# Attention and two expert layers on one core: where a step's scores, first products and setup stand in the issue order

## The chip, the core and the metric

The kernel runs on one NeuronCore of a Trainium2 chip. It uses TensorE (PE; weight loads are listed apart as PEld), VectorE (DVE), ScalarE (ACT), GpSimd (POOL) and SyncE (SP), whose queue issues most of the transfers. Each engine works through its own instructions in order and waits where an operand, or a buffer that it is to write, is not free. The metric is the device time of one execution in microseconds, median of three runs.

## What is computed

Sizes: 2 batches, 8 heads, 576 positions, head width 64; then 1152 tokens of width 512.

```python
def _attn_ref(q, k, v, tau):
    scores = q @ k.T / sqrt(64)
    thresh = max(scores, -1) - tau
    scores = where(scores >= thresh, scores, -1e9)
    attn = exp(scores - max(scores, -1))
    attn = attn / (sum(attn, -1) + 1e-09)
    return attn @ v
def _moe_ref(x, w_in, w_out):              # 512 -> 2048 -> 512
    h = x @ w_in
    return where(h > 0, h, exp(min(h, 0)) - 1) @ w_out
def _moe2_ref(x, w_gate, w1, w2, capacity):  # 8 experts, 512 -> 1024 -> 512
    e = argmax(x @ w_gate); gate = softmax(x @ w_gate)[e]
    # each token goes to its expert while that has room
    out = gate * (relu(x @ w1[e]) @ w2[e])
```

The three are chained: attention, its heads laid side by side as x, the first layer, the expert layer.

## The kernel before, in words

Every operand of a product is split into two float16 parts, a rounded one and the remainder; a product is three matmuls (high by high, high by low, low by high) into one PSUM sum. The rounded part is ACT's copy, the remainder a subtraction on VectorE or GpSimd.

**Attention** works in 36 steps, four for each of the nine tiles of 128 rows, a step for a pair of heads. Tile 4 lies across the two batches. In a step VectorE takes the two maxima from the scores in PSUM (`emit_max`, L267) and makes two limits of them (`nb` L268, `th` L269); ACT takes the exponentials (L273); VectorE masks them against the limits and sums rows (L279); ACT and GpSimd split the pair (`emit_split`, L288, L289); SP transposes it by DMA (`emit_pt`, L294, tile `pt`); two steps later TensorE multiplies it with the values (`emit_pv`, L311: the old step's product). The scores of the next step (`emit_s`, L245) go into the same two score buffers, so each head's scores must wait for the mask of the same head. At a tile's last pair `emit_x` normalises it (L324 to L335) and transposes it into `xt`.

Key tiles (`prep_k`, L212 on ACT, L213 on VectorE) and value tiles (`prep_v`, L107 and L108) are loaded and split in the steps before their use, for batch 0 at the start and for batch 1 around steps 15 to 20, into five buffers each. Query tiles are split in the third step of a tile.

**Under the steps lies the first layer.** `conv` turns one of 32 pieces of its weights, which arrive as 64-bit numbers, into float16 parts: three VectorE operations (L358 to L362), two copies on ACT (L369, L370) and a GpSimd subtraction (L371). `CONV` puts one into steps 0 and 1 and two into steps 2 to 16. `piece` emits a chunk of products: a first product (`mm1_chunk`, L386, 48 matmuls into the one bank `mma`) or a second (`mm2_chunk`, L418, 12 matmuls into `mmb`). `FILL` sets how many pieces a step gets: none before step 7, three to step 17, two after; `piece(2)` allows second products alone, `piece(1)` takes a first product where it can. A first product's bank is read by `after` in three stages that `flush` advances: ACT (L400, L401), VectorE (L403), then ACT and GpSimd (L407, L408). Finished rows are routed to experts by `route`, which `slot` advances a stage at a time (x2_hi L442, x2_lo L447, and small VectorE operations); rows go out by an indirect DMA of GpSimd (L498).

Inside the loop the order on each engine is that of the program (`manual_schedule`). It is, for step i: old product; key loads and key split; value loads; `flush(1)`; maxima, exponentials; `flush(1)`; one conversion; `flush(1)`; pieces; mask of head 0, **scores of head 0**, mask of head 1; split and transpose; `settle`; second conversion; `emit_x`; `slot`; last piece; **scores of head 1**; value split; query split. Ahead of the loop stand `setup_first`, the first loads, key 0 and query 0, and `setup_rest` (L152: load and split of the gate weights, L153 to L155, constants on GpSimd and VectorE), then the scores of step 0.

**After the loop** a planner orders the instructions. A loop emits what is left of the first layer, with the first expert weights prepared among it; the last tile gets its own path (L546 to L613). Then come the eight experts (L671, L727, L700), their 32 weight pieces of 1 MB each loaded by SP (L622) and split by ACT and VectorE (L631, L634).

Of the kernel before, what the change touches and what calls it, by code (L numbers as in the profile page):

```python
# [7 lines left out]
F16 = mybir.dt.float16  # L8
# [12 lines left out]
P = 128  # L21
# [20 lines left out]
def kernel(  # L42
# [95 lines left out]
    lnsc = const.tile([P, 1], F32, name="lnsc")  # L138

# [12 lines left out]
    def setup_rest():  # L152
        nc.sync.dma_start(out=wg_f, in_=w_gate)  # L153
        nc.scalar.activation(out=wg[:, 0], in_=wg_f, func=ACTF.Copy, scale=SC)
        nc.vector.scalar_tensor_tensor(  # L155
            out=wg[:, 1], in0=wg_f, scalar=SC, in1=wg[:, 0], op0=ALU.mult, op1=ALU.subtract
        )
        nc.gpsimd.memset(lnsc, LN_GS)
        nc.gpsimd.memset(zero, 0.0)
        nc.gpsimd.memset(cum, 0.0)  # L160
        nc.gpsimd.memset(ones, 1.0)
        nc.gpsimd.iota(ev_i, pattern=[[1, E]], base=-E, channel_multiplier=0)
        nc.vector.tensor_copy(ev, ev_i)
        nc.gpsimd.iota(ids, pattern=[[P, NTILE]], base=0, channel_multiplier=1)
        nc.vector.tensor_scalar(ids, ids, OOB_ID, None, ALU.bitwise_xor)

        nc.gpsimd.affine_select(
            out=tri, in_=ones, pattern=[[1, P]], compare_op=ALU.is_gt, fill=0.0,
            base=0, channel_multiplier=-1,
        )  # L170
# [37 lines left out]
    def prep_k(b, j):  # L208
        k2 = raw_t.pop(("k", b, j))
        kt = attn.tile([P, 2, S], F16, name="kst", tag="kst", bufs=5)  # L210
        flat = kt.rearrange("p h s -> p (h s)")
        nc.scalar.activation(out=flat[0:D], in_=k2, func=ACTF.Copy, scale=SC)  # L212
        nc.vector.scalar_tensor_tensor(  # L213
# [4 lines left out]
    def prep_v(b, j):  # L218
        v1 = raw_t.pop(("v", b, j))
        vt = attn.tile([P, 2, VC], F16, name="vst", tag="vst", bufs=5)  # L220
# [99 lines left out]
    def emit_x(t_):  # L320
# [3 lines left out]
        nc.vector.tensor_scalar(r, rs, 1e-9, SC / XS, ALU.add, ALU.mult)  # L324
# [9 lines left out]
        xt[t_] = moe1.tile([P, 8, P], F16, name="xt", tag="xt", bufs=6)  # L334
# [44 lines left out]
    def mm1_chunk(t_, q, bank):  # L379
        ps = ps_m.tile([P, 512], F32, name=f"mm{bank}", tag=f"mm{bank}")  # L380
# [42 lines left out]
    def mm2_done(ps, t_, q0, q1):  # L423
# [3 lines left out]
        elif q0 == 0:  # L427
            x2acc[t_] = shared.tile([P, DM], F32, name="acc", tag="acc", bufs=3)
# [378 lines left out]
    def pick2():  # L807
# [5 lines left out]
        for t_ in range(NTILE - 1):  # L813
# [5 lines left out]
            if ready("o", q + QG - 1, 6) and (q or aside < 3):  # L819
                return t_, q + QG  # L820
# [9 lines left out]
    def piece(first=0):  # L830
# [5 lines left out]
        if b is None or (a is not None and first < 2):  # L836
            q = nq1[a]
            nq1[a] += 1
            bank = "a"
            flush()  # L840
            evac.append(mm1_chunk(a, q, bank))
# [15 lines left out]
    cur, done = {}, []  # L857

# [12 lines left out]
    with tc.manual_schedule():  # L871
# [10 lines left out]
        prep_k(0, 0)  # L882
        prep_q(0)
        setup_rest()
        sc = {z: emit_s(0, z) for z in range(2)}
        for i in range(NSTEP + LAG):
# [3 lines left out]
            nf = FILL[i]  # L890
            if i >= LAG:
# [6 lines left out]

            for b, base in ((0, 0), (1, 4 * NPAIR)):
# [3 lines left out]
                if 0 <= jk < NPAIR:  # L903
                    prep_k(b, jk)
                jv = i + 1 - LAG - base
# [4 lines left out]
            flush(1)  # L910
            if on:
                lim = emit_max([sc[z] for z in range(2)])
                for z in range(2):
                    emit_exp(sc[z], lim[0], pair_p[i], z)
            flush(1)
            if nc_:
                conv_next()
            flush(1)
            for _ in range(nf - 1):
                piece(2) or (nc_ and not evac and piece(1))  # L920
            if on:
                for z in range(2):
                    emit_mask(sc[z], lim[1], pair_p[i], z, t_, 2 * j + z)
                    if z == 0 and i + 1 < NSTEP:
                        sc[0] = emit_s((i + 1) // NPAIR, (2 * i + 2) % H)
                emit_split(i)
                emit_pt(i)
            settle()
            for _ in range(nc_ - 1):
                conv_next()  # L930
            if i >= LAG and (i - LAG) % NPAIR == NPAIR - 1:
                emit_x((i - LAG) // NPAIR)
                x_at[(i - LAG) // NPAIR] = i
            slot()
            if nf:
                piece(1)
            if i + 1 < NSTEP:
                sc[1] = emit_s((i + 1) // NPAIR, (2 * i + 3) % H)
            for b, base in ((0, 0), (1, 4 * NPAIR)):
                jv = i + 1 - LAG - base  # L940
                if 0 <= jv < NPAIR:
                    prep_v(b, jv)
# [37 lines left out]
    k = 0  # L980
    while sum(nq1) < NQ * NTILE or sum(nq2) < NQ * (NTILE - 1) or evac:
# [143 lines left out]
```

## Time and profile before

| | us |
|---|---|
| median of three runs | 633.44 |
| lowest and highest run | 630.64, 633.81 |
| profiled execution | 635.48 |
| its span, first to last instruction | 633.7 |
| PE busy | 452.4 (71%) |
| DVE busy | 405.0 (64%) |
| ACT busy | 354.4 (56%) |
| POOL busy | 267.8 (42%) |

Busy time leaves out register, branch, semaphore and DMA-issuing instructions. The shares are means over stages with different limits, so they are read stage by stage further down. The span is shorter than the execution, since it runs from the first to the last instruction.

### The profile page before, as it was taken

The numbers are of one execution on the slowest core, as the hardware profiler recorded it, in microseconds if no ns is written. First come the engines' busy times: TensorE is split into PE (matmuls) and PEld (weight loads), VectorE is DVE, ScalarE is ACT, GpSimd is POOL, SyncE is SP. The second block draws the span as 40 slices with busy tenths as digits, with TensorE's granted clock in tenths as the row PEclk, the third lists the DMA queues.
The fourth block names the chain that finished last, engine by engine and source line by source line (L and its number), as shares of the span: only waits on it lengthen the run. The fifth ranks groups of instructions, "written<-read, shape, count | busy, mean of one in ns | idle before, by whom it ended". The sixth has DMA issues, their size and how long they took to land.

```text
span 633.7 us, 13023 instructions
## 1 busy us (share of the span) xinstructions
PE 452.4 (71%) x5343; PEld 367.6 (58%) x5343; DVE 405.0 (64%) x768; ACT 354.4 (56%) x511; POOL 267.8 (42%) x193
## 2 busy tenths in 40 slices
PE   1123345754654678995899899976989999787793
PEld 0012234444523636773677677654889999787681
DVE  2588795894596576785779578366534567654541
ACT  2346456565556456654576756366538665675541
POOL 1225446364455163453555455321234244533342
PEclk9999997776878789997999899989999999998898
DMA  6465677477456665853589747496617897887731
GB/s 190 140 147 159 171 185 182 113 185 200 104 139 173 162 151 141 193 124 72 109 179 212 118 94 102 88 291 223 228 45 206 245 283 242 241 276 210 236 67 41
DMA packets 150771, 105.59 MB, mean 167 GB/s; under 512 B 135209, under 2 KB 135209, under 8 KB 146608
## 3 DMA queue, kind: packets, MB, share of 16 engines
q1 hardware_dynamic: 148064, 99.94, 62.1%
q0 software_dynamic: 2640, 4.74, 2.3%
q8 instruction: 44, 0.72, 0.5%
q14 instruction: 23, 0.19, 0.1%
HBM read 60.06 MB, written 12.68 MB: 115 GB/s over the span
## 4 chain that ended last, share of the span: by engine, by line
DVE 38%; DMA 22%; PE 16%; ACT 11%; issue 10%; POOL 2%; SPq 1%; DVEq 0%; POOLq 0%; ACTq 0%
DMA stg<-in_w_dram 8%; PE mma L386 8%; DVE pp L279 7%; DVE m L267 6%; DMA out_dram<-y,ix 5%; DVE cvp L359 4%; DVE we L634 3%; DVE cvp L358 3%; PE mmb L418 3%; DMA pt<-phl 3%; DMA yr<-yt 2%; DVE kst L213 2%; PE s L245 2%; ACT we L631 2%; DVE cvp L362 2%
## 5 line engine op out<-in xcount | busy, mean ns | idle before, releaser
L386 PE MATMUL mma<-xt,wi 128*128 128x128 f16 x1728 | 116.2, 233 | 33.1 <-DVE gf L403 33.1
L386 PEld LDWEIGHTS <-wi 128*128 128x128 f16 x1728 | 111.2, 106 | 37.1 <-issue 25.4
L245 PE MATMUL s<-kst,qst 128*128 128x288 f16 (+1 forms) x320 | 56.2, 333 | 72.5 <-DVE pp L279 63.4
L418 PE MATMUL mmb<-wo,g 128*128 128x512 f16 x384 | 95.8, 403 | 12.1 <-DVE x L447 6.5
L634 DVE SCALAR_TENSOR_TENSOR we<-stg,we 128x1024 f16<-128x1024 f32 x64 | 78.3, 1256 | 38.9 <-ACT we L631 38.7
L289 POOL TENSOR_TENSOR phl<-pp,phl 128x1152 f16<-128x1152 f32 x36 | 85.3, 2371 | 14.8 <-POOL g L408 9.2
L631 ACT ACTIVATE we<-stg 128x1024 f16<-128x1024 f32 x64 | 64.4, 1049 | 41.5 <-DMA stg<-in_w_dram 40.7
L408 POOL TENSOR_TENSOR g<-gf,g 128x512 f16<-128x512 f32 x36 | 41.7, 1157 | 102.6 <-ACT g L407 102.5
L273 ACT ACTIVATE pp<-s,nb,escale 128x576 f32<-128x576 f32 x72 | 55.9, 827 | 49.2 <-DVE nb L268 49.1
L245 PEld LDWEIGHTS <-qst 128*128 128x128 f16 (+1 forms) x320 | 29.4, 112 | 91.6 <-DVE pp L279 53.3
L671 PE MATMUL mm<-xs,we 128*128 128x196 f16 x768 | 69.6, 253 | 14.3 <-DVE g L754 4.8
L671 PEld LDWEIGHTS <-we 128*128 128x128 f16 x768 | 66.7, 100 | 16.2 <-DVE we L634 8.1
L418 PEld LDWEIGHTS <-g 128*128 128x128 f16 x384 | 37.5, 103 | 56.7 <-issue 22.3
L311 PE MATMUL pv<-vst,pt 128*128 128x64 f16 (+3 forms) x1080 | 48.5, 208 | 30.7 <-DVE xf L327 11.9
L267 DVE TENSOR_REDUCE m<-s 128x1 f32<-128x576 f32 x72 | 52.0, 750 | 27.0 <-PE s L245 26.7
L311 PEld LDWEIGHTS <-pt 128*128 128x128 f16 (+1 forms) x1080 | 46.2, 108 | 37.1 <-issue 30.5
L684 POOL TENSOR_TENSOR ht<-rf,ht 128x392 f16<-128x392 f32 x32 | 35.7, 1126 | 74.3 <-issue 38.7
L727 PE MATMUL mm<-ht,we 128*128 128x196 f16 x672 | 58.5, 248 | 2.0 <-DVE yt L738 1.3
L727 PEld LDWEIGHTS <-we 128*128 128x128 f16 x672 | 57.4, 98 | 2.4 <-issue 2.3
L279 DVE SCALAR_TENSOR_TENSOR pp<-s,th,pp 128x576 f32<-128x576 f32 x72 | 55.9, 813 | 4.4 <-ACT pp L273 4.3
L288 ACT ACTIVATE phl<-pp 128x1152 f16<-128x1152 f32 x36 | 41.9, 1165 | 12.7 <-DVE pp L279 12.7
L400 ACT ACTIVATE ef<-mma 128x512 f32<-128x512 f32 x36 | 21.4, 594 | 46.3 <-PE mma L386 42.1
(123 smaller groups left out, 599.5 us busy)
## 6 DMA issues: line engine op xcount, KB each, us to landing
stg<-in_w_dram SPq DMA_DIRECT2D x32, 1024.0 KB, 6.4
cst<-in_w_in_dram SPq DMA_DIRECT2D x16, 512.0 KB, 4.4
cst<-in_w_out_dram SPq DMA_DIRECT2D x16, 512.0 KB, 4.4
disp<-zero SPq DMA_DIRECT2D x6, 771.0 KB, 4.7
qraw<-in_qt_dram SPq DMA_DIRECT2D x9, 512.0 KB, 3.4
vraw<-in_vb_dram SPq DMA_DIRECT2D x8, 320.0 KB, 5.7
kraw<-in_kt_dram SPq DMA_DIRECT2D x8, 288.0 KB
out_dram<-zero SPq DMA_DIRECT2D x1, 2304.0 KB
```

Of the source, the lines that this page charges most:

```text
L245: nc.tensor.matmul(s[a:z, half, 0:288], q2[:, pas, h, a:z], kst[b, h // 2][:, h % 2, half * 288:(half + 1) * 288], start=(pas == 0), stop= ...
L267: nc.vector.tensor_reduce(out=m[:, z:z + 1], in_=sc[z], axis=AX.XY, op=ALU.max)
L273: nc.scalar.activation(out=pp[:, z].rearrange("p (a c) -> p a c", a=2), in_=s, func=ACTF.Exp, bias=nb[:, z:z + 1], scale=escale,)
L279: nc.vector.scalar_tensor_tensor(out=e, in0=s, scalar=th[:, z:z + 1], in1=e, op0=ALU.is_ge, op1=ALU.mult, accum_out=rsum[t_][:, h:h + 1],)
L289: nc.gpsimd.tensor_tensor(out=d[:, 1], in0=flat, in1=d[:, 0], op=ALU.subtract)
L311: nc.tensor.matmul(o[a:e, h:h + w // D, :].rearrange("p h d -> p (h d)"), q[:, ph * 9 + blk, a:e], vt[:, vh, c:c + w], start=(blk == 4 and ...
L386: nc.tensor.matmul(ps[:, o * P:(o + 1) * P], w[:, wh, kk, :], xt[t_][:, xh * 4 + kk, :], start=(k_ == 0), stop=(k_ == 11),)
L418: nc.tensor.matmul(ps, gt[t_, q][:, gh, o, :], w[:, wh, :], start=(first and o == 0 and n == 0), stop=(last_ and o == QF - 1 and n == 2),)
L631: nc.scalar.activation(out=w[:, 0, part], in_=t[:, part], func=ACTF.Copy, scale=SC)
L634: nc.vector.scalar_tensor_tensor(out=w[:, 1, part], in0=t[:, part], scalar=SC, in1=w[:, 0, part], op0=ALU.mult, op1=ALU.subtract)
L671: nc.tensor.matmul(ps[:, o * n:(o + 1) * n], w[:, wh, kk % 2, f * P:(f + 1) * P], t[:, xh * 4 + kk, :], start=(k_ == 0), stop=(k_ == 11),)
L727: nc.tensor.matmul(ps[:, o * n:(o + 1) * n], w[:, wh, f % 4, j * P:(j + 1) * P], h2[:, gh, f, :], start=(f == 0 and n_ == 0), stop=(f == 7 ...
```

## The change

- **Scores.** Head 0's scores stay behind its mask, and head 1's now follow head 1's mask directly, ahead of everything else on TensorE.
- **Pieces.** Ahead of the masks only second products are emitted (`piece(2)`, without the fallback to a first product); one first product, `piece(1)`, ends the step. The stages of its reader are emitted once behind the exponentials and then, all that are left, behind the split and the transpose.
- **Keys and values.** Both get six buffers. The key split's ACT half stays at the head of a step, its VectorE half moves behind the exponentials. Values are loaded and split one step earlier.
- **Setup.** `setup_rest` moves from ahead of the first scores to the end of step 0, behind its split, transpose and `settle`. It gets two more constants, `eps` and `xsc`, which L324 reads in place of immediates.
- **Order of the rest.** The second conversion of a step moves behind `emit_x`.
- **After attention** a first product takes one of five rotating banks (`ps_e`, `mm`) in place of `mma`.
- **Buffers.** `xt` goes from six to four, `acc` from three to two, and two tiles at most (not three) may have a partial second product set aside.

```diff
@@ setup_rest
         nc.gpsimd.memset(lnsc, LN_GS)
+        nc.gpsimd.memset(eps, 1e-9)
+        nc.gpsimd.memset(xsc, SC / XS)
@@ prep_k (prep_v: bufs=5 to bufs=6)
-        kt = attn.tile([P, 2, S], F16, name="kst", tag="kst", bufs=5)
+        kt = attn.tile([P, 2, S], F16, name="kst", tag="kst", bufs=6)
         flat = kt.rearrange("p h s -> p (h s)")
         nc.scalar.activation(out=flat[0:D], in_=k2, func=ACTF.Copy, scale=SC)
+        yield
         nc.vector.scalar_tensor_tensor(
@@ emit_x (xt: bufs=6 to bufs=4; acc in mm2_done: bufs=3 to bufs=2)
-        nc.vector.tensor_scalar(r, rs, 1e-9, SC / XS, ALU.add, ALU.mult)
+        nc.vector.tensor_scalar(r, rs, eps, xsc, ALU.add, ALU.mult)
@@ mm1_chunk
-        ps = ps_m.tile([P, 512], F32, name=f"mm{bank}", tag=f"mm{bank}")
+        ps = bank()
@@ pick2
-            if ready("o", q + QG - 1, 6) and (q or aside < 3):
+            if ready("o", q + QG - 1, 6) and (q or aside < 2):
@@ piece
-            evac.append(mm1_chunk(a, q, bank))
+            evac.append(mm1_chunk(a, q, m1_bank[0]))
@@ ahead of the loop
+    m1_bank = [lambda: ps_m.tile([P, 512], F32, name="mma", tag="mma")]
...
-        prep_k(0, 0)
+        for _ in prep_k(0, 0):
+            pass
         prep_q(0)
-        setup_rest()
-        sc = {z: emit_s(0, z) for z in range(2)}
+        sc = [emit_s(0, z) for z in range(2)]
@@ the loop
+            halves = []
             for b, base in ((0, 0), (1, 4 * NPAIR)):
...
                 if 0 <= jk < NPAIR:
-                    prep_k(b, jk)
-                jv = i + 1 - LAG - base
+                    halves.append(prep_k(b, jk))
+                jv = i - base
...
-            flush(1)
+            for g in halves:
+                next(g)
             if on:
-                lim = emit_max([sc[z] for z in range(2)])
+                lim = emit_max(sc)
                 for z in range(2):
                     emit_exp(sc[z], lim[0], pair_p[i], z)
+            for g in halves:
+                next(g, None)
             flush(1)
             if nc_:
                 conv_next()
-            flush(1)
             for _ in range(nf - 1):
-                piece(2) or (nc_ and not evac and piece(1))
+                piece(2)
             if on:
                 for z in range(2):
                     emit_mask(sc[z], lim[1], pair_p[i], z, t_, 2 * j + z)
-                    if z == 0 and i + 1 < NSTEP:
-                        sc[0] = emit_s((i + 1) // NPAIR, (2 * i + 2) % H)
+                    if i + 1 < NSTEP:
+                        sc[z] = emit_s((i + 1) // NPAIR, (2 * i + 2 + z) % H)
                 emit_split(i)
                 emit_pt(i)
+            flush()
             settle()
-            for _ in range(nc_ - 1):
-                conv_next()
             if i >= LAG and (i - LAG) % NPAIR == NPAIR - 1:
                 emit_x((i - LAG) // NPAIR)
                 x_at[(i - LAG) // NPAIR] = i
+            if i == 0:
+                setup_rest()
+            for _ in range(nc_ - 1):
+                conv_next()
             slot()
             if nf:
                 piece(1)
-            if i + 1 < NSTEP:
-                sc[1] = emit_s((i + 1) // NPAIR, (2 * i + 3) % H)
             for b, base in ((0, 0), (1, 4 * NPAIR)):
-                jv = i + 1 - LAG - base
-                if 0 <= jv < NPAIR:
-                    prep_v(b, jv)
+                if 0 <= i - base < NPAIR:
+                    prep_v(b, i - base)
@@ after the loop
+    m1_bank[0] = lambda: ps_e.tile([P, 512], F32, name="mm", tag="mm")
```

## Rows read from the trace of the kernel before

**Rows 1.** Windows, four stretches: length, busy us per engine (instructions), clock, DMA share, GB/s.

```profile
0.00:99.60 99.60, 30.35 (x274) 20.91 (x274) 71.05 (x120) 47.53 (x63) 36.88 (x33) 1.00 0.60 163
99.60:245.24 145.64, 88.61 (x964) 66.33 (x964) 99.89 (x172) 80.33 (x117) 68.78 (x46) 0.79 0.64 163
245.24:391.48 146.24, 131.00 (x1769) 98.45 (x1770) 109.38 (x250) 93.09 (x128) 77.57 (x46) 0.96 0.65 128
391.48:470.75 79.27, 65.86 (x850) 52.91 (x849) 42.07 (x118) 40.68 (x63) 23.05 (x20) 0.94 0.64 180
```

**Rows 2.** Waits of the whole span: who waited for whom, us in total, times, longest.

```profile
PE s L245 <- DVE pp L279: 63.4, 19, 16.0
...
PE mma L386 <- DVE gf L403: 33.1, 10, 5.3
...
DVE m L267 <- PE s L245: 26.7, 13, 5.5
```

**Rows 3.** Timeline, first masks of steps 0, 1, 6, 7, 8, 18, 35: start, us.

```profile
26.41 0.81 DVE L279 SCALAR_TENSOR_TENSOR pp<-s,th,pp 128x576 f32<-128x576 f32 x1
...
36.63 0.81 DVE L279 SCALAR_TENSOR_TENSOR pp<-s,th,pp 128x576 f32<-128x576 f32 x1
...
91.23 0.81 DVE L279 SCALAR_TENSOR_TENSOR pp<-s,th,pp 128x576 f32<-128x576 f32 x1
...
99.60 0.81 DVE L279 SCALAR_TENSOR_TENSOR pp<-s,th,pp 128x576 f32<-128x576 f32 x1
...
116.16 0.81 DVE L279 SCALAR_TENSOR_TENSOR pp<-s,th,pp 128x576 f32<-128x576 f32 x1
...
245.24 0.82 DVE L279 SCALAR_TENSOR_TENSOR pp<-s,th,pp 128x576 f32<-128x576 f32 x1 [0.24 <-ACT pp L273]
...
391.48 0.82 DVE L279 SCALAR_TENSOR_TENSOR pp<-s,th,pp 128x576 f32<-128x576 f32 x1 [0.25 <-ACT pp L273]
```

**Rows 4.** Groups by line, whole span: busy us, mean ns, idle before and its releaser.

```profile
L267 DVE TENSOR_REDUCE m<-s 128x1 f32<-128x576 f32 x72 | 52.0, 750 | 27.0 <-PE s L245 26.7
...
L403 DVE SCALAR_TENSOR_TENSOR gf<-ef,mma 128x512 f32<-128x512 f32 x36 | 24.6, 682 | 17.5 <-ACT ef L401 17.4
...
L268 DVE TENSOR_SCALAR nb<-m,cmul 128x2 f32<-128x2 f32 x36 | 15.5, 430 | 1.3
...
L213 DVE SCALAR_TENSOR_TENSOR kst<-kraw,kst 64x1152 f16<-64x1152 f32 x8 | 13.0, 1626 | 22.7 <-ACT kst L212 22.6
```

**Rows 5.** Timeline of the start, SP's queue and ACT: start, us, idle before.

```profile
8.12 0.47 SPq L195 DMA_DIRECT2D kraw<-in_kt_dram  x1
...
19.93 0.23 ACT L154 ACTIVATE wg<-wg_f 128x32 f16<-128x32 f32 x1 [12.16 <-DMA wg_f<-in_w_gate_dram]
...
31.64 2.84 SPq L294 DMA_TRANSPOSE pt<-phl  x1
```

**Rows 6.** Chain of waits, first load: start, us.

```profile
1.27 4.24 DMA kraw<-in_kt_dram
```

**Rows 7.** Timeline, step 7's second first product: start, us, idle before.

```profile
106.36 5.28 PE L386 MATMUL mma<-xt,wi 128*128 128x128 f16 x48 [5.14 <-DVE gf L403]
```

**Rows 8.** Timeline near 120 us, GpSimd's subtraction and VectorE's two limits.

```profile
119.68 2.36 POOL L289 TENSOR_TENSOR phl<-pp,phl 128x1152 f16<-128x1152 f32 x1
...
121.14 0.93 DVE L268 TENSOR_SCALAR nb<-m,cmul 128x2 f32<-128x2 f32 x1
...
121.98 1.20 DVE L269 TENSOR_SCALAR th<-m,cadd 128x2 f32<-128x2 f32 x1
```

**Rows 9.** Timeline of TensorE, the old step's product in steps 24 and 25.

```profile
300.90 1.03 PE L311 MATMUL pv<-vst,pt 128*128 128x128 f16 x27
...
308.07 1.03 PE L311 MATMUL pv<-vst,pt 128*128 128x128 f16 x27
```

**Rows 10.** Timeline of ACT at step 22: start, us, idle before.

```profile
290.44 0.60 ACT L442 ACTIVATE x<-mmb 128x512 f16<-128x512 f32 x1 [8.52 <-DMA disp<-x,slot_i]
```

**Rows 11.** Waits from 405 to 470 us: us in total, times, longest.

```profile
PE mma L386 <- DVE gf L403: 7.8, 4, 3.5
```

More of the change, by code (lines that the diff above doesn't have):

```diff
@@ L138 @@
     lnsc = const.tile([P, 1], F32, name="lnsc")
+    eps = const.tile([P, 1], F32, name="eps")
+    xsc = const.tile([P, 1], F32, name="xsc")
     def setup_first():
@@ L219, in prep_v @@
         v1 = raw_t.pop(("v", b, j))
-        vt = attn.tile([P, 2, VC], F16, name="vst", tag="vst", bufs=5)
+        vt = attn.tile([P, 2, VC], F16, name="vst", tag="vst", bufs=6)
         split(vt[:, 0], vt[:, 1], v1, SC, "dve")
@@ L333, in emit_x @@
         nc.gpsimd.tensor_tensor(out=xh[:, 1], in0=xf, in1=xh[:, 0], op=ALU.subtract)
-        xt[t_] = moe1.tile([P, 8, P], F16, name="xt", tag="xt", bufs=6)
+        xt[t_] = moe1.tile([P, 8, P], F16, name="xt", tag="xt", bufs=4)
         nc.sync.dma_start_transpose(out=xt[t_], in_=xh.rearrange("p a s -> p (a s)"))
@@ L427, in mm2_done @@
         elif q0 == 0:
-            x2acc[t_] = shared.tile([P, DM], F32, name="acc", tag="acc", bufs=3)
+            x2acc[t_] = shared.tile([P, DM], F32, name="acc", tag="acc", bufs=2)
             nc.scalar.activation(out=x2acc[t_], in_=ps, func=ACTF.Copy)
@@ L838, in piece @@
             nq1[a] += 1
-            bank = "a"
             flush()
-            evac.append(mm1_chunk(a, q, bank))
+            evac.append(mm1_chunk(a, q, m1_bank[0]))
             g_at[a, q] = step[0] + 1
```

## The prediction

> **What bounds the kernel now.** I first cut the span at the starts of the first mask of steps 0, 1, 6, 7, 8, 18 and 35 [rows 3] and read the busy time of each engine between the cuts [rows 1]. The reader is to see four stages with different limits, and an expert stage behind them. In steps 0 to 7 VectorE works 71.1 of 99.6 us and TensorE 30.4: the vector chain decides. In steps 7 to 18 (145.6 us for 11 steps, 13.2 each) nobody is full: VectorE 99.9, TensorE 88.6, at a granted clock of 0.79. In steps 18 to 35 (146.2 us, 8.6 each) TensorE is near full with 131.0. In the tail up to the first expert product TensorE has 65.9 of 79.3 us.
>
> Then I read who waits [rows 2]. TensorE waits 63.4 us for masks before scores and 33.1 us for the vector step that frees the only bank of a first product; VectorE waits 26.7 us for scores. The second stage shows how these hang together: step 7 puts two first products around the scores. The second of them begins 5.1 us late, since its bank is freed behind VectorE's work, then runs at half the full clock (5.28 us for 48 products, against about 2.7 at 2.4 GHz, half of it) [rows 7], and the second head's scores stand behind it on TensorE. The step from 99.60 to 116.16 takes 16.6 us, while the step before it, with two weight conversions and no product, takes 8.4 [rows 3].
>
> **Start and steps 0 to 7.** Now the gate-weight load is last in SP's first batch, and ACT's copy of it at 19.93 us holds everything [rows 5]. After the change it goes behind step 0. The second key tile is issued at 8.12 [rows 5]; a key load took 4.24 us [rows 6], so it is there at 12.4. From the release at 19.93 to the mask at 26.41 passed 6.5 us; the maxima and their two limits (two of 0.75 us [rows 4], the limits some 0.3 more) no longer come behind the keys, the gate copy is 0.2, so the first mask starts near 12.4 + 4.5 = 16.9, 9.5 earlier. But the moved step is not free. On SP it stands behind step 0's transpose, which is issued 5.2 us after the mask begins (26.41 to 31.64) and holds the queue 2.84 [rows 3, 5]; with a landing of 4.24 [rows 6] the gate weights are there at 16.9 + 5.2 + 2.8 + 4.2 = 29.1. ACT and VectorE wait there in order, and behind them the value pieces, which the change also puts one step earlier (0.7 on ACT, 0.8 on VectorE, estimates by length from the key piece of 1.63 [rows 4]), and the next maxima. The 6.5 us then serve again, less the key copy on ACT (about 1.1, now beside the maxima), plus these 1.5: the second mask at 36.0, against 36.63 [rows 3]. So 9 of the 9.5 us are given back. A landing in half the time would leave 2 more, in twice the time cost 4. I take 1 gained: 4.24 is the nearest row, but for 18 times the bytes. GpSimd's nine small setup operations, two more than before, fill its wait behind step 0's subtraction. Step 4 has no value piece any more: it falls from about the 10.9 that steps 1 to 6 average to the plain 8.4 of step 6 now [rows 3], a gain of 2.4; the tile's normalisation, now ahead of a conversion and so ahead of GpSimd's subtraction, gives 0.6 (an estimate). **Stage: -4**, bounds +4 and -8.
>
> **Steps 7 to 18.** With at most one first product in a step, always behind both scores, its bank's reader runs straight behind the masks and no score stands behind a product. That leaves VectorE's loop. Base: nine steps at 8.37 [rows 3]; the last two lack one and two conversions of some 2.05 (8.37 less two maxima of 0.75 [rows 4], two masks that follow each other as fast, and 1.2 of limits with their waits, halved): 6.3 and 4.3. Sum 85.9. Eight steps carry a product's reader, 0.68 [rows 4], and 0.6 because its subtraction on GpSimd lies before the limits: 10.2. Three normalisations, 1.1 each by the size of their one long operation: 3.3. Four key pieces at 1.63 [rows 4]: 6.5; each of them waited for ACT at the head of its step and now lies under the exponentials, and with six buffers the copy need not wait for the scores of the oldest keys. Two value pieces with their waits, 1.8 each: 3.6. One accumulator addition and a row split, 2, and collisions with GpSimd's query pieces, 3, are estimates. Total 114.5 against 145.6. **Stage: -31.** Were TensorE at half clock throughout, a first product of 5.28 [rows 7] and twice the 1.03 of an old step's product [rows 9], and as much again for the scores, are 9.5, still beside VectorE's 9.65; only the three steps with second products would grow, by some 10 together. Bounds: -38 (no collision, no wait of limits) and -11 (every step 2 us more).
>
> **Steps 18 to 35.** TensorE's round is 7.17 us, from one step's old product to the next's [rows 9]; no product is added or taken, so it stays. What changes is the slack. Before, the first maximum was taken under the first product. Now maxima follow the masks at once and the limits come due about 2.2 us after them (a product's reader and two maxima [rows 4]), while GpSimd's 2.36-us subtraction of the step runs: in step 0 the transpose behind it was issued 3.7 us after the two masks [rows 3, 5], so it runs from 1.3 to 3.7. The rows show what that means: a limit begun at 121.14, in the last us of such a subtraction, took 0.93 and ended with it, and the next limit then took 1.20, until the following GpSimd operation ended [rows 8]. So the first limit ends 3.9 us after the masks, the second 5.0, behind the product's subtraction, and two masks of 0.75 spacing end at 6.6. Add 0.15 for ACT. 6.75 against 7.17 leaves 0.4, and whatever VectorE does between masks and maxima now counts against it. Eight steps with routing, value or query work then cost about 0.5 more: **+4**, bounds -8 (the old order's own excess halves) and +17 (1 us in every step). The long wait of step 22 (ACT 8.5 us for a dispatched row [rows 10]) stays: the same tiles are routed in the same steps, and fewer transposed tiles or accumulators bind nowhere, since their last reader is at least six steps earlier.
>
> A page of the Trainium skill speaks against this part: SBUF — State Buffer, section Who interferes with whom, says that a two-port VectorE operation and a GpSimd operation exclude each other, the later one blocked until the earlier has finished, and that issue order decides. The trace agrees as to the exclusion, 0.93 and 1.20 us for limits of which the first kind takes 0.43 on the mean of 36; as to the order, the first limit slipped in between two GpSimd operations here.
>
> **Tail and experts.** Counting the pieces through, attention ends with 29 first products done, not 30, so the tail gets one more: +2.7. Taking five rotating banks there removes the 7.8 us that products waited for their bank's reader [rows 11]. **-5**; bounds +3 (none of it removed) and -11 (all 13.4 us of TensorE's idle time gone [rows 1]). The weight loads start when attention ends and so move with it. The order of this part is a planner's; what it does with the experts I set at 0, within 6 either way. Constants from tiles instead of immediates: nothing, since the limits, of the same operation, read their scalar from a tile already.
>
> **How the numbers follow.** -4 - 31 + 4 - 5 = -36 against a profiled execution of 635.5 (633.7 of span, 1.8 around): 599.5. The median of the runs is 2.0 below it: **597.5**, in its own range 588 to 607. Chance 0.50.
>
> **Rivals.** (a) VectorE's limits bind the third stage: if the product's subtraction on GpSimd goes ahead of the first limit as well, as the 1.20 us of the second show it can [rows 8], the loop is 6.75 + 1.2 = 7.95, 0.78 over TensorE's round, 13 us in 17 steps: 610. For it: GpSimd is at work 77.6 of 146 us there [rows 1]; against it, the limit that slipped in [rows 8]. By the page's rule on issue order, named above, it would come out so. 0.18. (b) Only stalls that hang on the second product go: the second stage keeps other waits (loads, ACT's order), 20 us of the 31 stay: 617. For it: all waits of first products for their bank are 33.1 us, in the whole kernel [rows 2], so that 31 asks for nearly everything; against it, the plain step of 8.4 with the same loads [rows 3]. That is also how it looks if the change doesn't do what it says. 0.12. (c) The tail loses all its idle time, and the third stage runs at TensorE's round: 6 and 10 more: 581. 0.13. (d) Slower: without a product between the scores, TensorE's cover of the mask chain is gone; when everything that VectorE does between masks and limits also waits for GpSimd, the third stage's loop sets the pace. It eats the gain of 40 elsewhere from 7.17 + 40/17 = 9.5 us per step on; at 9.8 it gives 638. Against it: that needs 3 us more than the loop I find. 0.07.
>
> A difference of 0.5%, 3 us, is about what a measurement of this kernel can tell from none. Faster 0.91, same 0.02 (the far end of (b)), slower 0.07. The range of 8 in 10 takes in (c), (a) and most of (b): 580 to 618.
>
> **What would show it.** First masks of steps 0, 1, 7, 18 and 35 near 17, 36, 95.5, 210 and 360; the gate copy near 29; waits of first products for their bank near nil, and of maxima for scores too; the mean of the first limit up from 0.43 [rows 4] to over 1 us. Wrong is the forecast if the second stage stays over 125 us, if the third passes 160, or if the experts take 10 us more than their 163.

## The result and the profile after

The changed kernel takes 599.15 us (median of four runs, 597.22 to 601.08), the kernel before 633.11 on the same occasion (630.64 to 633.81): ratio 0.947, 95% interval 0.943 to 0.951. The profiled execution took 600.27, its span 598.6. The forecast was 597.5, in a range from 580 to 618.

The first view is the windows of after, cut at the first masks of steps 7, 18 and 35 and at the first expert product, as [rows 1] cut before (columns: stretch, its length, busy time and count of each engine, granted clock, DMA share, GB/s):

```profile
core 0: us, PE busy (x) PEld busy (x) DVE busy (x) ACT busy (x) POOL busy (x), PEclk, DMA share, GB/s
0.00:93.21 93.21, 26.33 (x226) 18.40 (x226) 69.97 (x120) 47.39 (x63) 36.86 (x35) 0.82 0.61 175
93.21:207.07 113.86, 77.51 (x899) 54.63 (x900) 102.45 (x172) 77.96 (x113) 67.61 (x45) 0.86 0.75 198
207.07:359.11 152.04, 136.92 (x1835) 101.80 (x1836) 116.30 (x248) 89.40 (x127) 76.96 (x46) 0.97 0.58 131
359.11:432.29 73.18, 65.91 (x897) 53.99 (x896) 43.29 (x120) 42.77 (x68) 26.70 (x21) 0.95 0.64 193
432.29:598.60 166.31, 140.73 (x1491) 132.44 (x1488) 83.68 (x112) 92.89 (x143) 60.43 (x49) 0.93 0.71 196
```

The second stage lost 31.8 of its 145.6 us, and VectorE is now busy for 90% of it, against 69%. The third stage got 5.8 us longer. The other stages moved by -6.4 (start), -6.1 (tail) and +3.4 (experts).

The cuts, and two steps more, are the first masks of steps 0, 1, 7, 8, 18 and 35 (start, duration), as in [rows 3]:

```profile
16.40 0.82 DVE L284 SCALAR_TENSOR_TENSOR pp<-s,th,pp 128x576 f32<-128x576 f32 x1
32.92 0.82 DVE L284 SCALAR_TENSOR_TENSOR pp<-s,th,pp 128x576 f32<-128x576 f32 x1
93.21 0.81 DVE L284 SCALAR_TENSOR_TENSOR pp<-s,th,pp 128x576 f32<-128x576 f32 x1
101.57 0.81 DVE L284 SCALAR_TENSOR_TENSOR pp<-s,th,pp 128x576 f32<-128x576 f32 x1
207.07 0.82 DVE L284 SCALAR_TENSOR_TENSOR pp<-s,th,pp 128x576 f32<-128x576 f32 x1
359.11 0.82 DVE L284 SCALAR_TENSOR_TENSOR pp<-s,th,pp 128x576 f32<-128x576 f32 x1 [0.85 <-ACT pp L278]
```

Step 7 takes 8.36 us instead of 16.56. The waits of the whole span (us in total, times, longest), as in [rows 2]: TensorE's for a first product's bank are down from 33.1 to 4.6, VectorE's for scores from 26.7 to 6.4. TensorE waits longer for masks than before (82.1 against 63.4), which costs nothing where VectorE sets the pace.

```profile
PE s L250 <- DVE pp L284: 82.1, 19, 14.4
PE mma L391 <- DVE gf L408: 4.6, 9, 1.3
DVE m L272 <- PE s L250: 6.4, 4, 4.8
```

The groups of the maxima and limits (count | busy, mean ns | idle before), as in [rows 4]: the first limit went from a mean of 0.43 us to 0.64, the second from 0.30 to 0.66.

```profile
L272 DVE TENSOR_REDUCE m<-s 128x1 f32<-128x576 f32 x72 | 50.9, 747 | 6.4 <-PE s L250 6.4
L274 DVE TENSOR_SCALAR th<-m,cadd 128x2 f32<-128x2 f32 x36 | 23.6, 655 | 0.0
L273 DVE TENSOR_SCALAR nb<-m,cmul 128x2 f32<-128x2 f32 x36 | 22.9, 637 | 1.3
```

### The profile page after: what moved, and what is told of

Same layout as the page of the kernel before. It is cut to its first block, busy times and chain, and to the rows that moved or that the text cites. A ratio compares the mean times of both kernels' runs of the same rounds, so it can differ in the third digit from the quotient of the medians.

```text
span 598.6 us, 13017 instructions
## 1 busy us (share of the span) xinstructions
PE 447.4 (75%) x5343; PEld 361.3 (60%) x5343; DVE 415.7 (69%) x768; ACT 350.4 (59%) x511; POOL 268.6 (45%) x195
## 4 chain that ended last, share of the span: by engine, by line
DVE 39%; DMA 21%; issue 12%; ACT 12%; PE 12%; POOL 2%; SPq 1%; DVEq 0%; POOLq 0%; ACTq 0%
DMA stg<-in_w_dram 9%; DVE m L272 6%; DVE pp L284 6%; PE mma L391 4%; DVE we L639 4%; PE mmb L423 4%; DMA yr<-yt 4%; DVE cvp L364 4%; DVE cvp L363 3%; ACT pp L278 3%; DMA out_dram<-y,ix 3%; ACT we L636 2%; DVE gf L408 2%; DVE nb L273 2%; DMA disp<-x,slot_i 2%
## 5 line engine op out<-in xcount | busy, mean ns | idle before, releaser
L250 PE MATMUL s<-kst,qst 128*128 128x288 f16 (+1 forms) x320 | 54.1, 330 | 91.6 <-DVE pp L284 82.1
L391 PEld LDWEIGHTS <-wi 128*128 128x128 f16 x1728 | 103.5, 101 | 9.7 <-issue 6.9
L639 DVE SCALAR_TENSOR_TENSOR we<-stg,we 128x1024 f16<-128x1024 f32 x64 | 79.5, 1276 | 37.8 <-ACT we L636 37.5
L391 PE MATMUL mma<-xt,wi 128*128 128x128 f16 x1392 | 87.2, 225 | 4.7 <-DVE gf L408 4.6
L676 PE MATMUL mm<-xs,we 128*128 128x196 f16 x768 | 73.9, 261 | 13.3 <-DVE g L759 5.0
L676 PEld LDWEIGHTS <-we 128*128 128x128 f16 x768 | 70.3, 104 | 15.8 <-DVE we L639 8.0
L284 DVE SCALAR_TENSOR_TENSOR pp<-s,th,pp 128x576 f32<-128x576 f32 x72 | 55.9, 814 | 11.0 <-ACT pp L278 10.2
L413 POOL TENSOR_TENSOR g<-gf,g 128x512 f16<-128x512 f32 x36 | 45.1, 1254 | 34.4 <-ACT g L412 34.3
L732 PEld LDWEIGHTS <-we 128*128 128x128 f16 x672 | 57.4, 98 | 1.8 <-issue 1.7
L316 PE MATMUL pv<-vst,pt 128*128 128x64 f16 (+3 forms) x1080 | 45.0, 204 | 1.9 <-DVE xf L332 1.9
L316 PEld LDWEIGHTS <-pt 128*128 128x128 f16 (+1 forms) x1080 | 42.8, 106 | 3.8 <-issue 2.3
L376 POOL TENSOR_TENSOR wi<-cv,wi 128x512 f16<-128x512 f32 x16 | 18.5, 1158 | 55.1 <-ACT cv L375 55.1
```

The lines of the kernel that those rows point to most:

```text
L250: nc.tensor.matmul(s[a:z, half, 0:288], q2[:, pas, h, a:z], kst[b, h // 2][:, h % 2, half * 288:(half + 1) * 288], start=(pas == 0), stop= ...
L284: nc.vector.scalar_tensor_tensor(out=e, in0=s, scalar=th[:, z:z + 1], in1=e, op0=ALU.is_ge, op1=ALU.mult, accum_out=rsum[t_][:, h:h + 1],)
L316: nc.tensor.matmul(o[a:e, h:h + w // D, :].rearrange("p h d -> p (h d)"), q[:, ph * 9 + blk, a:e], vt[:, vh, c:c + w], start=(blk == 4 and ...
L391: nc.tensor.matmul(ps[:, o * P:(o + 1) * P], w[:, wh, kk, :], xt[t_][:, xh * 4 + kk, :], start=(k_ == 0), stop=(k_ == 11),)
L639: nc.vector.scalar_tensor_tensor(out=w[:, 1, part], in0=t[:, part], scalar=SC, in1=w[:, 0, part], op0=ALU.mult, op1=ALU.subtract)
L676: nc.tensor.matmul(ps[:, o * n:(o + 1) * n], w[:, wh, kk % 2, f * P:(f + 1) * P], t[:, xh * 4 + kk, :], start=(k_ == 0), stop=(k_ == 11),)
```

## The experiments

All twelve kernels are cut like the two above; a step runs from its first mask to the next step's. Each line has the median, then from the profiled execution the first mask of step 7, the second and third stage, tail and experts, in us.

| kernel | median | step 7 at | 7 to 18 | 18 to 35 | tail | experts |
|---|---|---|---|---|---|---|
| before | 633.1 | 99.6 | 145.6 | 146.2 | 79.3 | 162.9 |
| before, one first product a step | 625.5 | 99.6 | 132.6 | 145.4 | 82.5 | 162.5 |
| before, both scores early | 623.1 | 99.8 | 138.8 | 144.7 | 75.5 | 162.8 |
| before, with both of these | 617.4 | 99.3 | 126.9 | 146.3 | 82.3 | 163.2 |
| after | 599.2 | 93.2 | 113.9 | 152.0 | 73.2 | 166.3 |
| after, two first products allowed | 601.3 | 93.9 | 117.2 | 149.3 | 75.4 | 162.8 |
| after, head 1's scores late | 624.8 | 93.9 | 122.8 | 166.4 | 72.2 | 167.2 |
| after, reader early | 599.3 | 94.0 | 124.9 | 144.0 | 75.5 | 164.0 |
| after, keys as before | 606.6 | 95.2 | 121.7 | 150.4 | 74.5 | 164.0 |
| after, one bank in the tail | 608.8 | 93.4 | 113.3 | 152.0 | 83.1 | 162.7 |
| after, gate weights in step 3 | 597.6 | 92.7 | 114.2 | 152.0 | 72.4 | 164.1 |
| after, limits on ACT | 573.8 | 87.6 | 104.5 | 141.8 | 75.2 | 164.3 |
| the same, setup taken apart | 570.3 | 82.5 | 105.1 | 142.4 | 75.3 | 163.9 |
| the same, two first products | 571.8 | 82.6 | 109.2 | 139.4 | 76.5 | 163.3 |

Kernels with the same tail differ there by up to 4 us (79.3 and 75.5; 72.2 to 75.5), and the experts, which no edit touches, by 4.7. No reading below rests on less than that in these two columns.

### One first product, and early scores, in the kernel before

```diff
-                piece(2) or (nc_ and not evac and piece(1))
+                piece(2)
```

> The kernel before, with one edit: a step no longer takes a first product in place of a second one, so that steps 7, 11, 12 and 15 have one first product instead of two; head 1's scores stay behind that product. Theory 1 (what costs is the product that starts late in front of head 1's scores): steps 7, 11, 12 and 15 together fall by about 25 us, the second stage goes from 145.6 to about 120, the tail gets a first product more (+2.7): 610, within 4. Rival (a product in front of head 1's scores costs by itself, so both edits are needed): at most half of it, 620 or more.

Measured: 0.990 of before (0.986 to 0.994). Steps 7, 11 and 12 fall by 6.8, 5.9 and 5.1 us, but step 15 by only 0.5, and steps 8, 9, 13, 14 and 16 rise by 5.2 together, as the refused products move to later steps. Of Theory 1's 25 us 13.0 are left in the stage. One product in front of head 1's scores still costs, as the third run below shows (126.9 against 132.6).

```diff
-                    if z == 0 and i + 1 < NSTEP:
-                        sc[0] = emit_s((i + 1) // NPAIR, (2 * i + 2) % H)
+                    if i + 1 < NSTEP:
+                        sc[z] = emit_s((i + 1) // NPAIR, (2 * i + 2 + z) % H)
...
-            if i + 1 < NSTEP:
-                sc[1] = emit_s((i + 1) // NPAIR, (2 * i + 3) % H)
```

> The kernel before, with one edit: head 1's scores directly behind their mask, as head 0's. The second first product stays, and so does the bank's reader, ahead of the masks, its first operation on ACT ahead of the exponentials. Theory (the place of the scores carries most of the second stage): second stage 145.6 to about 123, third stage about the same, 608 to 614. Rival (the reader has to move behind the masks too, since ACT now waits for the product in front of the exponentials): second stage over 132, 620 or more.

Measured: 0.983 (0.978 to 0.989); step 7 is as long as ever (16.12). The rival's figures came out: moving the scores alone is not enough. Its reason holds in part only. In step 7 the second first product still begins 4.5 us late for its bank, and VectorE waits 4.7 us for the reader behind it; with one product a step (the next run) step 7 falls to 10.98, though the reader still stands ahead of the masks.

> The kernel before, with two edits: head 1's scores directly behind their mask, and no first product in place of a second one. The first alone took 6.8 us off the second stage, the other 13.0. Theory (the two do not only add, since one product that starts late still stands in front of head 1's scores, or two in front of the reader): second stage about 122, what the keys' edit gives (7.8) above the changed kernel's 114: 606 to 610. Rival (they add or overlap, and the reader's place and the keys bring the rest): second stage 126 or more, 612 to 620.

Measured: 0.975 (0.970 to 0.980). Second stage -18.7, about the sum of -13.0 and -6.8: they add, and 13 us are still missing to the changed kernel. The rival's figures hold; the reader and the keys, taken back below, are looked at for those 13.

### Each part taken back out of the changed kernel

Second first products allowed again (the first diff above, reversed; three steps take one):

> The changed kernel, with the second first product allowed again; it then comes in steps 7, 11 and 15, the first of the two ahead of both heads' scores and the other behind both. Theory 1 (only scores behind a late product cost): 1 to 2 us in each of the three steps, the tail gets 2.7 back: 598 to 604. Rival, as the prediction has it (a second product in a step costs as such, whatever stands behind it): about 8, 8 and 5 us, 615 to 620.

Measured: 0.954 (0.948 to 0.960); the interval overlaps the changed kernel's. Steps 7 and 11 are 2.9 us longer each, step 15 1.5 shorter. Theory 1's sum holds: with both scores ahead of the second product it costs 3.3 us in the stage, not 21. The 2.7 us come back in the third stage and not in the tail (75.4 against 73.2, within that column's spread). What it costs is a wait: in steps 7 and 11 the reader of the first product stands ahead of the second, ACT comes to it only behind the split, and VectorE is idle for 2.47 us before its own part. Step 7 of this kernel:

```profile
95.53 1.17 ACT L293 ACTIVATE phl<-pp 128x1152 f16<-128x1152 f32 x1 [0.38 <-DVE pp L284]
96.60 0.58 ACT L405 ACTIVATE ef<-mma 128x512 f32<-128x512 f32 x1
97.97 0.69 DVE L408 SCALAR_TENSOR_TENSOR gf<-ef,mma 128x512 f32<-128x512 f32 x1 [2.47 <-ACT ef L406]
```

Head 1's scores back behind the last piece (the second diff, reversed):

> The changed kernel, with head 1's scores back behind the step's last product. Prediction's account (the third stage lost 5.8 us since limits come sooner and fall under GpSimd's subtraction): the third stage falls from 152.0 to 146 to 148; the second, where each product now stands once more in front of head 1's scores, rises by 1 us in each of some eight steps, 114 to about 122: 597 to 604. Rival (the order of the scores does nothing in the third stage, other edits lost it): the third stage stays at 152, 605 to 608.

Measured: 0.988 (0.985 to 0.991), 25 us over the changed kernel, and the worst miss of the study: the third stage did not fall to 147 but rose to 166. Neither account had the reason. In the changed kernel the bank's reader stands behind the masks, so a product can begin only after them, and scores behind that product wait for both. The waits of its third stage show it:

```profile
PE mma L391 <- DVE gf L408: 13.1, 11, 2.6
DVE m L272 <- PE s L250: 15.9, 9, 5.5
```

Before, the reader stood ahead of the masks, and there the place of the scores makes next to no difference to the third stage: with one product a step it takes 145.4 us with late scores and 146.3 with early ones. The place of the scores and that of the reader are one decision.

The reader in its old three places:

```diff
             for g in halves:
                 next(g)
+            flush(1)
...
                 conv_next()
+            flush(1)
...
                 emit_pt(i)
-            flush()
```

> The changed kernel, with the reader of a first product's bank back in its three places ahead of the masks (ACT's part ahead of the limits, VectorE's behind the exponentials, the rest behind the conversion). Prediction's account (the reader straight behind the masks is a part of the second stage's gain, since ahead of the exponentials ACT waits for the product): second stage from 113.9 to 122 or more; third 146 to 148, since the limits no longer stand behind the reader: 600 to 606. Rival (with both scores ahead of the product the reader's place is free in the second stage and costs in the third): second stage within 3 of 114, third 145 to 147: 590 to 596.

Measured: 0.946 (0.940 to 0.951), no change in the whole: the median is 599.3 against 599.2 (the profiled execution, 604.1, was the longest of its four). The prediction's account gives both stages right in sign (second 124.9, +11.0; third 144.0, -8.0). In the second stage ACT has the reader's first operation ahead of the exponentials and waits there for the product, 18.5 us in seven places; ahead of step 8's masks it looks like this (start, duration, [idle before and what ended it]):

```profile
101.28 0.60 ACT L405 ACTIVATE ef<-mma 128x512 f32<-128x512 f32 x1 [2.59 <-PE mma L391]
101.91 0.72 ACT L406 ACTIVATE ef<-ef,lnsc 128x512 f32<-128x512 f32 x1
102.54 1.53 ACT L278 ACTIVATE pp<-s,nb,escale 128x576 f32<-128x576 f32 x2
102.67 0.69 DVE L408 SCALAR_TENSOR_TENSOR gf<-ef,mma 128x512 f32<-128x512 f32 x1 [2.32 <-ACT ef L406]
```

So the reader's new place wins in one stage what it loses in the other. No run had it late in the second stage and early in the third; by the -8.0 of the third that would be some 591 us (an estimate).

The keys as before:

```diff
-        kt = attn.tile([P, 2, S], F16, name="kst", tag="kst", bufs=6)
+        kt = attn.tile([P, 2, S], F16, name="kst", tag="kst", bufs=5)
...
-        yield
         nc.vector.scalar_tensor_tensor(
...
         kst[b, j] = kt
+        yield
```

> The changed kernel, with the keys as before: five buffers, and VectorE's half of a key piece at the head of its step, directly behind ACT's half, ahead of the maxima. Prediction's account (the half waits for ACT there, and lies under the exponentials now): about 1 us more in steps 0 to 2 each, 6 to 8 us more in steps 14 to 17, 607 to 610. Rival (those waits of the kernel before were the late scores' alone, which are gone in any case): 599 to 603.

Measured: 0.957 (0.952 to 0.963), 7.5 us over the changed kernel. Steps 14 to 17 are 1.7, 1.4, 1.8 and 2.9 longer, 7.8 together, as expected; steps 0 to 2 don't change, against the expectation, but the first mask comes at 18.3 instead of 16.4. The edit takes back two things at once, the sixth buffer and the half's place, and no run separates them. The longest wait, in the kernel with old keys, is for the scores that still read the oldest of five buffers:

```profile
184.50 1.16 ACT L216 ACTIVATE kst<-kraw 64x1152 f16<-64x1152 f32 x1 [4.09 <-PE s L250]
185.70 1.35 DVE L217 SCALAR_TENSOR_TENSOR kst<-kraw,kst 64x1152 f16<-64x1152 f32 x1 [6.41 <-ACT kst L216]
```

One bank in the tail:

```diff
-    m1_bank[0] = lambda: ps_e.tile([P, 512], F32, name="mm", tag="mm")
```

> The changed kernel, with the one bank for first products kept in the tail. Prediction's account (the rotating banks took out the 7.8 us for which first products waited there): the tail rises from 73.2 to about 81, 605 to 608. Rival (the tail fell because more of it was hidden, or the bank's reader is not what ended last): tail within 2 us of 73, 598 to 601.

Measured: 0.964 (0.960 to 0.967). The tail is 9.9 us longer; products wait 10.8 us for the bank in it. The first line is of this kernel's tail, the second of the changed kernel's:

```profile
PE mma L391 <- DVE gf L408: 10.8, 5, 4.6
...
PE mma L391 <- DVE gf L408: 1.3, 1, 1.3
```

### The setup

```diff
     def setup_rest():
-        nc.sync.dma_start(out=wg_f, in_=w_gate)
...
                 load_conv(len(stage_t))
+        nc.sync.dma_start(out=wg_f, in_=w_gate)
...
-            if i == 0:
+            if i == 3:
                 setup_rest()
```

> The changed kernel; the gate weights' load is now last in SP's first batch, as in the kernel before, and everything that uses it (the copies, constants and fills of the setup) comes behind step 3 instead of step 0. Prediction's account (step 0 lasts 16.5 us because ACT and VectorE wait for that load): step 0 takes about 11, the first mask stays at 16.5, all else moves up by 5: 593 to 596. Rival (another load, of keys or values, is due there as well): at most 2 us, 597 to 600.

Measured: 0.944 (0.938 to 0.949), 1.6 below the changed kernel, with overlapping intervals: the median lies in the rival's range, but not for its reason. Step 0 falls from 16.52 to 11.08, as expected: it was the load. But step 3 rises from 10.74 to 15.67. There VectorE's small half of the gate weights (0.19 us in step 0) is held for 2.39 until GpSimd's subtraction ends, and the next copy then waits for GpSimd's fills:

```profile
53.21 2.37 POOL L293 TENSOR_TENSOR phl<-pp,phl 128x1152 f16<-128x1152 f32 x1 [0.45 <-POOL wo L375]
53.23 2.39 DVE L156 SCALAR_TENSOR_TENSOR wg<-wg_f,wg 128x32 f16<-128x32 f32 x1 [1.35 <-ACT wg L155]
56.88 0.17 DVE L166 CAST ev<-ev_i 128x8 f32<-128x8 int32 x1 [1.25 <-POOL ev_i L165]
```

### The limits on ACT, and a faster kernel

```diff
-        nc.vector.tensor_scalar(nb, m, cmul, None, ALU.mult)
-        nc.vector.tensor_scalar(th, m, cadd, None, ALU.add)
+        nc.scalar.activation(out=nb, in_=m, func=ACTF.Copy, scale=cmul)
+        nc.scalar.activation(out=th, in_=m, func=ACTF.Identity, bias=cadd)
```

> The changed kernel, with both limits taken by ACT (two operations of some 0.2 us in front of the exponentials) instead of VectorE. Prediction's account (a limit on VectorE is held until GpSimd's subtraction ends; th took 1.20 us in nearly every step from 5 to 15, nb 1.8 to 2.2 in steps 18, 22 and 26): about 1 us less in each of some ten steps of the second stage and two of the first, 4 to 6 us less in the third, 582 to 589. Rival (VectorE's next operation is held in its place, or ACT's longer queue takes the gain): 596 to 602.

Measured: 0.905 (0.898 to 0.911), 25 us below the changed kernel and more than expected: -5.2 in steps 1 to 7, -9.4 in the second stage, -10.2 in the third. Two lines of the changed kernel's step 7 and, below, three of this kernel's show why: the second limit was held until GpSimd's subtraction ended at 99.59, and the next conversion on VectorE came behind it; now the limits go past the same subtraction on ACT, and the conversion begins directly behind the maxima. Holding is not all of it: two limits at their shortest are 0.45 us of VectorE's time in every step, some 5 us in the second stage, and what they took beyond that in the changed kernel is 4.0, 10.7 and 16.0 us in the three stages. No run separates the two.

```profile
98.41 1.20 DVE L274 TENSOR_SCALAR th<-m,cadd 128x2 f32<-128x2 f32 x1
98.43 1.16 POOL L376 TENSOR_TENSOR wo<-cv,wo 128x512 f16<-128x512 f32 x1
...
92.65 0.68 DVE L363 TENSOR_SCALAR cvp<-cst 128x512 int32<-128x512 int32 x1
92.84 1.16 POOL L376 TENSOR_TENSOR wo<-cv,wo 128x512 f16<-128x512 f32 x1
92.97 0.28 ACT L274 ACTIVATE th<-m,cadd 128x2 f32<-128x2 f32 x1
```

Then the setup taken apart as well: GpSimd's constants and fills at the very start, the gate weights' load last in the first batch, ACT's copy of them ahead of step 2's limits, VectorE's half ahead of its masks.

```diff
     def setup_rest():
-        nc.sync.dma_start(out=wg_f, in_=w_gate)
-        nc.scalar.activation(out=wg[:, 0], in_=wg_f, func=ACTF.Copy, scale=SC)
-        nc.vector.scalar_tensor_tensor(
-            out=wg[:, 1], in0=wg_f, scalar=SC, in1=wg[:, 0], op0=ALU.mult, op1=ALU.subtract
-        )
...
         setup_first()
+        setup_rest()
...
                 load_conv(len(stage_t))
+        nc.sync.dma_start(out=wg_f, in_=w_gate)
...
+            if i == 2:
+                nc.scalar.activation(out=wg[:, 0], in_=wg_f, func=ACTF.Copy, scale=SC)
             if on:
                 lim = emit_max(sc)
...
+            if i == 2:
+                nc.vector.scalar_tensor_tensor(
+                    out=wg[:, 1], in0=wg_f, scalar=SC, in1=wg[:, 0], op0=ALU.mult, op1=ALU.subtract
+                )
...
-            if i == 0:
-                setup_rest()
```

> The changed kernel with the limits on ACT, and the setup taken apart: constants and fills at the very start, where GpSimd has nothing to do, the gate weights' load last in SP's first batch, their two copies in step 2 ahead of the masks. Prediction's account of the start (step 0 waits for that load; the 4.9 us that came back behind step 3 were GpSimd's fills and its subtraction): step 0 takes 11 instead of 16.1 and nothing comes back, 567 to 570. Rival (it comes back in another step once more): 572 to 575.

Measured: 0.901 (0.897 to 0.906). Step 0 takes 10.8, VectorE's half 0.19 us, and nothing comes back: the first mask of step 7 stands at 82.5 instead of 87.6. The median falls by 3.5 us, less than the 5.1 of that stage, to a value between the two forecasts, and the two intervals overlap. This is the fastest kernel of the study, 29 us below the changed one.

And the second first product allowed in it, by the first diff of the section, reversed:

> As the kernel with limits on ACT and the setup taken apart, with the second first product allowed again in steps 7, 11 and 15. Alone that edit gave 3.3 us to the second stage and took 2.7 off the third and 1.3 off tail and experts. Theory (the second stage's price was VectorE's, which now has 1.4 us less to do in a step): 1 to 4 us below the kernel without it, 564 to 568. Rival (the price is TensorE's, at half clock): the same or slower, 568 to 573.

Measured: 0.903 (0.899 to 0.908). The second stage pays 4.1 and the third gives 3.0 back, about as in the changed kernel: the theory that VectorE's fullness set the price falls. The rival's sum came out, but TensorE's clock isn't the reason either: the same wait stands in step 7 (and 11) as in the changed kernel, 2.47 us of VectorE for ACT's part of the reader, which with the reader's own 0.69 is about the 3.0 us that each of the two steps grows by.

```profile
85.29 0.58 ACT L400 ACTIVATE ef<-mma 128x512 f32<-128x512 f32 x1
86.66 0.69 DVE L403 SCALAR_TENSOR_TENSOR gf<-ef,mma 128x512 f32<-128x512 f32 x1 [2.47 <-ACT ef L401]
```

## Why the prediction was right, and where it was not

**Total.** The terms were -4, -31, +4, -5 and 0 (-36); the spans give -6.4, -31.8, +5.8, -6.1 and +3.4 (-35.1). The signs of the four terms hold, and each lies within its bounds; the reasons hold unevenly. That the median came within 1.7 us of the forecast is in part luck: the errors of the five terms, -2.4, -0.8, +1.8, -1.1 and +3.4, cancel to +0.9.

**Start: the landing was mis-sized.** The first mask came at 16.4 (16.9 forecast), step 4 fell by 2.4 as forecast. The wait for the gate weights is the named one, but it was sized by a key load of 4.24 us [rows 6]: the load was issued at 23.86 and let ACT go at 26.00, 2.1 later. It was also issued 1.0 us sooner than counted (16.9 + 5.2 + 2.8 = 24.9). So 6.3 us were given back, not 9, and the second mask stands at 32.9 instead of 36.0; two of these 3.1 us are the case "a landing in half the time" of the forecast.

```profile
23.86 0.57 SPq L155 DMA_DIRECT2D wg_f<-in_w_gate_dram  x1
26.00 0.23 ACT L156 ACTIVATE wg<-wg_f 128x32 f16<-128x32 f32 x1 [6.84 <-DMA wg_f<-in_w_gate_dram]
```

**Second stage: the size holds, but the weights of the parts don't.** Taken back one at a time out of the changed kernel, the ban on a second product is worth 3.3 us, the early scores 8.9, the reader behind the masks 11.0, the keys 7.8: 31.0 together. That this is near the whole 31.8 doesn't show that they add: the reader and the keys make 18.8, while 13 us were missing to the kernel with the other two. The new places of the value tiles and of the second conversion and the smaller buffers were not taken back. The prediction opened with the second product of step 7, and rival (b), that only the stalls on it go, had 11 of the 31 us; alone it brought 13.0. That it hardly matters once the scores and the reader are in place is what the prediction did not see. The step base of 8.37 was right (8.35 to 8.37 in steps 6, 7, 10 and 11), though the step it was read from was not without a product, as the prediction has it: a first product began there at 95.34, and only its reader fell into the next step.

**Third stage: +4 forecast, +5.8 measured, for the reason given in part, in other places.** The forecast had the limits end 3.9 and 5.0 us after the two masks and the next masks come 6.75 after the last. Step 24 does just that: its masks end at 270.46, the limits at 274.42 and 275.54, the next mask begins 6.74 after the one at 268.91.

```profile
272.02 2.38 POOL L294 TENSOR_TENSOR phl<-pp,phl 128x1152 f16<-128x1152 f32 x1 [4.71 <-issue]
272.99 1.43 DVE L273 TENSOR_SCALAR nb<-m,cmul 128x2 f32<-128x2 f32 x1
274.34 1.20 DVE L274 TENSOR_SCALAR th<-m,cadd 128x2 f32<-128x2 f32 x1
274.36 1.16 POOL L413 TENSOR_TENSOR g<-gf,g 128x512 f16<-128x512 f32 x1
275.65 0.82 DVE L284 SCALAR_TENSOR_TENSOR pp<-s,th,pp 128x576 f32<-128x576 f32 x1
```

But only 4 of the 17 steps take that 6.74. So "the mean of the first limit over 1 us" was wrong (0.64), and the loss lies elsewhere: steps 18, 22, 23 and 26 are 2.3, 1.0, 1.4 and 3.0 longer. There VectorE has the reader first, and what follows it, a routing operation or the first limit, falls under a subtraction of GpSimd. In step 26 `oh` takes 2.24 instead of the 0.35 it took in the same step before, and the limit 2.17 under the query's subtraction:

```profile
287.75 2.37 POOL L294 TENSOR_TENSOR phl<-pp,phl 128x1152 f16<-128x1152 f32 x1 [3.46 <-issue]
287.90 2.24 DVE L466 TENSOR_SCALAR oh<-ev,amin 128x8 f16<-128x8 f32 x1
...
293.08 2.17 DVE L273 TENSOR_SCALAR nb<-m,cmul 128x2 f32<-128x2 f32 x1
293.10 2.13 POOL L105 TENSOR_TENSOR qst<-qraw,qst 128x1024 f16<-128x1024 f32 x1 [1.87 <-ACT qst L104]
```

With the reader early these steps lie within 0.5 us of before. It is the held limits behind a late reader that cost, and not the holding alone: beyond their shortest the limits took 16.0 us in the changed kernel's third stage, and with the reader early still 13.6, in a stage 8.0 us shorter. The 5.8 also hide a gain of 2.2 in step 30 (11.0 before), which each edit of the kernel before brings as well (8.5) and which stays unexplained; without it the loss is the 8.0 that the reader's old place gives back. The round of 7.17 was no floor for one step either: with the limits on ACT step 24 takes 5.33 and step 25 9.23; so TensorE may bound the mean of the steps (132.5 busy of 141.8 us), but no single one. Step 22 keeps its wait, as forecast (18.1 us, ACT 9.0 for the dispatched row).

**The rivals.** (a), that the limits bind, did not come out as priced: it put 13 us on top of the +4, a third stage of some 163, and 152.0 was measured. Its mechanism is there all the same: moving the limits took 10.2 off the third stage, to 4.4 below the kernel before. What both missed is that the limits cost as much in the second stage (9.4), where `th` took 1.20 us in each of steps 6 to 14: the base step of 8.37 had contained such a limit all along.

The Trainium skill (SBUF — State Buffer, section Who interferes with whom), which the prediction weighed, says that ACT never waits for another engine's port; the trace agrees: on ACT the limits took 0.29 and 0.28 us on the mean, beside the same subtractions. On whether issue order decides, the rows are too close to tell (98.41 and 98.43 above).

**Tail: right.** Seven first products of 36 are left to it instead of six, as counted. One product more without the rotating banks gives tails of 82.3 to 83.1 us, with them 72.2 to 75.5; so the banks are worth 6.8 or more, against the 7.8 read from the waits [rows 11].

**Experts: +3.4, within the 6 allowed.** TensorE is busy 4.1 us longer there (140.7 against 136.6) for the same products, at a granted clock of 0.93 instead of 0.96. In the 10 us from 512.29 it is 0.66, behind a gap of 3.3 us in which TensorE waited for VectorE. It lies within the spread of kernels that share this stage, and was not followed further.

## What to carry to other kernels

A consumer's scores, the product behind them and the reader that frees the product's bank are one chain: decide their places together, and stage by stage. Alone, one product a step and early scores brought 13.0 and 6.8 of the second stage's 31.8 us; scores behind the product cost 25 us once the reader stood behind the masks; and the reader's new place won 11.0 us in the second stage and lost 8.0 in the third, so that on the median it brought nothing. Small operations on a full VectorE are dear where they fall under a GpSimd operation that holds them, so look for instructions whose mean lies far above their shortest duration, and try them on ACT first. Moving a setup step out of the way pays only if each engine's part of it goes to a place where that engine is idle.

## What was not expected of the hardware

- A limit of 128 x 2 elements takes 0.22 us on VectorE alone and up to 2.18 when a GpSimd subtraction runs; maxima and conversions, which read or write PSUM, keep their 0.75 and 0.70 us beside the same subtractions. Two such limits a step were worth 25 us of 599 to the kernel, more than any part of the change taken back but the late scores, which cost as much.
- The gate weights' small load landed 2.1 us after its issue, in half of the 4.24 of a key tile (one row each, the key tile's of the kernel's first load).
